# Padding stores one per step of the expert loop, and more buffers for its token numbers, gates and results

## The chip, the cores and the metric

The kernel runs on one core of one Trainium2 chip. The core's engines are TensorE (PE, with PEld for its weight loads), VectorE (DVE), ScalarE (ACT), GpSimd (POOL) and SyncE (SP, which here only issues transfers). Each engine works through its own instructions in order. The metric is the time of one execution in microseconds (us), and lower is better.

## What is computed

A Fourier mixer over 8 x 3072 tokens of width 256, a dense layer pair with a squared ReLU, and a layer of 8 experts in which each token goes to the one expert with the largest logit. The change touches the last part only:

```
def _moe2_ref(x, w_gate, w1, w2):
    logits = x @ w_gate
    expert_idx = np.argmax(logits, axis=1)
    probs = softmax(logits)                      # written out in the reference
    gate_w = probs[np.arange(N), expert_idx]
    for e in range(E):
        mask = expert_idx == e
        xe = x[mask]
        h = np.maximum(xe @ w1[e], 0.0)
        ye = h @ w2[e]
        out[mask] = gate_w[mask, None] * ye
```

N is 24,576 tokens, the width D is 256, E is 8 and the inner width of an expert is 1024. All is float32; the matmuls work on a high and a low part of each operand, three products to a matmul.

## The kernel before

The kernel has three stages that follow one another: the Fourier mixer, the dense layers, and the expert loop. The dense stage ends each tile of 384 tokens by computing the logits and writing each token's row to a table in DRAM, `bucket`, in the region of its expert. A row has 258 numbers: the 256 values, the gate, and the token's number. The region of an expert is filled from its start, so its last block of rows is only partly used.

The expert loop (`run`, L954) works on **slots**. A slot is a block of 512 rows of one expert (`ngr(s)` is 4, slots 0 to 40) or of 256 rows (`ngr(s)` is 2, slots 41 and on). A slot is worked in 4 or 2 **steps**. Each step of the loop does this, in program order:

- `e1` of the next step: the first expert matmuls, then ScalarE's `hh` (L872) and VectorE's `hl` (L873), the high and low parts of the hidden layer;
- one step of the side work (`_step(side)`, L959), until that is used up;
- on the first step of slot s: `prep_2(s + 1)`, the split of the second weights of the next slot, and `load(s + 3)`;
- `e2` of this step: the second expert matmuls (L892 to L894) into `acc`;
- on the last step of slot s: the results and their stores (below), then `prep_x(s + 2)` and `prep_1(s + 2)`.

`load(s)` issues three transfers on SyncE's queue: the slot's rows `xr` from `bucket` (L806), and the expert's weights `r1` (L812) and `r2` (L813). `prep_x(s)` copies the token numbers and gates out of `xr` on VectorE (`ids`, L823, and `gate`, L824), transposes the rows on TensorE and splits them. `ids` and `gate` come from the pool `p3`, which has three buffers for each name, so the copies for a slot take the buffers of three slots before.

The results of a slot are scaled by the gates on ScalarE into `ot` (L900). They go out by four (or two) indirect stores on GpSimd, one for each 128 rows (L902), which read `ot` and, as addresses, `ids`. `ot` shares its buffers with the `pay` of the dense stage; the pool `p2` has two of them.

The side work is one generator, `finish()`. It does the last tile of the dense stage (`gen_r`), then `table2` works out which rows the remaining slots hold, and ends with 16 **padding stores** (L746): indirect stores on GpSimd, two for each expert, that write 128 rows of `pad` each behind the last row of an expert's region. A padding row has a token number out of range, so that its result is not stored. Between the padding stores the generator yields after every second one, so that each step of the expert loop makes two. They write `bucket`, which the row loads read: a padding store waits for the one before it and for the row load issued before it, and a row load waits for the padding stores issued before it. The 16 stores are issued from the last step of slot 4 to the third step of slot 6.

Of the kernel before, what the change touches and what calls it, by code (L numbers as in the profile page):

```python
# [9 lines left out]
F32 = mybir.dt.float32  # L10
F32R = mybir.dt.float32r
F16 = mybir.dt.float16
I32 = mybir.dt.int32
# [6 lines left out]
D = 256  # L20
P = 128
# [6 lines left out]
ROW = D + 2  # L28
# [107 lines left out]
def kernel(  # L136
# [15 lines left out]
    def f32(ap):  # L152
        return ap.bitcast(F32)
# [52 lines left out]
    def ring():  # L206
        return psum["r"].tile([P, 512], F32, tag="r", name="r")
# [4 lines left out]
    def acc_tile():  # L212
        return psum["a"].tile([P, 1024], F32, tag="acc", name="acc")
# [322 lines left out]
    def x_tiles(k):  # L536
        p = spool["x"]
        xts[k] = (p.tile([P, 2, 512], F32R, tag="xth", name="xth"), p.tile([P, 2, 512], F32R, tag="xtl", name="xtl"))
        return xts[k]
# [42 lines left out]
    def moe():  # L582
# [4 lines left out]
        p2 = es.enter_context(tc.tile_pool(name="m2", bufs=2))  # L587
        p3 = es.enter_context(tc.tile_pool(name="m3", bufs=3))
# [63 lines left out]
        def row(name):  # L652
            return crow(name)[0:1]

        def tt(nm, shape):
            return p1.tile([1] + shape, F32, tag="tb_" + nm, name="tb_" + nm)
# [4 lines left out]
        def cumsum(dst, src):  # L661
            ltri = row("ltri").rearrange("o (a b) -> o a b", a=E)
            tmp = tt("tmp", [E, E])
            V.tensor_tensor(out=tmp, in0=ltri, in1=bc(src, 1, [E, E]), op=ALU.mult)
            V.tensor_reduce(out=dst, in_=tmp, axis=AX.X, op=ALU.add)

        def count(dst, src, thr, op):
            n = rowmap[thr][1]
            big = tt("big", [E, rowmap["thr"][1]])[:, :, 0:n]
            V.tensor_tensor(out=big, in0=bc(src, 2, [E, n]), in1=bc(row(thr), 1, [E, n]), op=op)  # L670
            V.tensor_reduce(out=dst, in_=big, axis=AX.X, op=ALU.add)
# [26 lines left out]
        def take(dst, avail, n):  # L698
            cum = tt("cum", [E])
            lim = tt("lim", [E])  # L700
            cumsum(cum, avail)
            V.tensor_scalar(out=lim, in0=cum, scalar1=float(n), scalar2=None, op0=ALU.min)
            V.tensor_copy(dst, lim)
            V.tensor_sub(dst[:, 1:E], lim[:, 1:E], lim[:, 0:E - 1])
            return lim
# [11 lines left out]
        def table2():  # L717
            te = tabs["te"]
            cnt, f, t2 = tt("cnt", [E]), tt("f", [E]), tt("t2", [E])
            V.tensor_sub(cnt, rbase[0:1], row("ecap"))  # L720
            count(f, cnt, "thr2", ALU.is_ge)
            yield
            V.tensor_sub(f, f, te)
            lim = take(t2, f, nf - nf1)
            yield
            yield from table(lim, t2, te, row("jf")[:, 0:nf - nf1], 512, nf1)
            V.tensor_add(te, te, t2)
            hc = tt("hc", [E])
            yield
            count(hc, cnt, "thr", ALU.is_gt)  # L730
            V.tensor_scalar(out=t2, in0=te, scalar1=-2.0, scalar2=None, op0=ALU.mult)
            V.tensor_add(hc, hc, t2)
            cum = tt("cum", [E])
            cumsum(cum, hc)
            V.tensor_scalar(out=slot_i[:, 2 * NS:2 * NS + 1], in0=cum[:, E - 1:E], scalar1=float(nf), scalar2=None, op0=ALU.add)
            yield
            yield from table(cum, hc, te, row("kh"), 256, nf)
            pf = p1.tile([P, E, 2], F32, name="padf", tag="padf")
            V.tensor_tensor(out=pf, in0=rbase.unsqueeze(2).to_broadcast([P, E, 2]),
                            in1=pidx.unsqueeze(1).to_broadcast([P, E, 2]), op=ALU.add)  # L740
            pint = p1.tile([P, 2 * E], I32, name="padi", tag="padi")
            V.tensor_copy(pint, pf.rearrange("p e i -> p (e i)"))
            for i in range(2 * E):
                if i % 2 == 0:
                    yield
                G.indirect_dma_start(  # L746
                    out=bucket[:, :], out_offset=bass.IndirectOffsetOnAxis(ap=pint[:, i:i + 1], axis=0),
                    in_=pad, in_offset=None)
# [24 lines left out]
        def g2(n, i):  # L773
            _, gh, gl = hid.pop((n, i))
            if i == 0:
                accs[n] = acc_tile()
            acc = accs[n]
            for f in range(2):
                fc = 2 * i + f
                for g in range(3):  # L780
                    o = acc[:, g * D:(g + 1) * D]
                    lh, ll = (t[:, f, g * P:(g + 1) * P] for t in (gh, gl))
                    st = fc == 0 and g != 1
                    T.matmul(o, lhsT=lh, rhs=woh[:, fc], start=st, stop=False, skip_group_check=True)  # L784
                    T.matmul(o, lhsT=lh, rhs=wol[:, fc], start=False, stop=False, skip_group_check=True)  # L785
                    T.matmul(o, lhsT=ll, rhs=woh[:, fc], start=False, stop=fc == 15, skip_group_check=True)  # L786
            if i == 7:
                pay = p2.tile([P, 4 * ROW], F32, tag="pay", name="pay")[:, :3 * ROW].rearrange("p (g c) -> p g c", g=3)
                acc = accs.pop(n)
                A.copy(pay[:, :, 0:D], acc[:, 0:3 * D].rearrange("p (g d) -> p g d", g=3))  # L790
                pays[n] = pay

        def ngr(s):
            return 4 if s < nf else 2

        def wset(s):
            hi, lo = (wih, woh) if s % 2 == 0 else (wil, wol)
            return hi[:, :, 0:F2], hi[:, :, F2:2 * F2], lo[:, 0:8], lo[:, 8:16]
# [17 lines left out]
        def prep_x(s, end):  # L816
            if s >= end:
                return
            k = ngr(s)
            xt = xr.pop(s)  # L820
            ids = p3.tile([P, 4], I32, tag="ids", name="ids")
            gate = p3.tile([P, 4], F32, tag="gate", name="gate")
            V.tensor_copy(ids[:, :k], xt[:, :, D + 1])  # L823
            V.tensor_copy(gate[:, :k], xt[:, :, D])  # L824
            meta[s] = ids, gate
            xh, xl = x_tiles(("s", s))
            for dc in range(2):
                ps = ring()
                for j in range(k):
                    T.transpose(ps[:, j * P:(j + 1) * P], xt[:, j, dc * P:(dc + 1) * P], ident)  # L830
                A.copy(xh[:, dc, :k * P], ps[:, :k * P])
                V.tensor_sub(xl[:, dc, :k * P], ps[:, :k * P], f32(xh[:, dc, :k * P]))
# [45 lines left out]
        def e2(s, i):  # L878
            k = ngr(s)
            nfc = 8 // k  # L880
            _, _, w2h, w2l = wset(s)
            hh, hl = (t.rearrange("p (f t) -> p f t", f=nfc) for t in hid.pop(("s", s, i)))
            if i == 0:
                accs["s", s] = acc_tile()
            acc = accs["s", s]
            for f in range(nfc):
                fc = nfc * i + f
                for g in range(k):
                    o = acc[:, g * D:(g + 1) * D]
                    lh, ll = (t[:, f, g * P:(g + 1) * P] for t in (hh, hl))  # L890
                    st = fc == 0 and g % 2 == 0
                    T.matmul(o, lhsT=lh, rhs=w2h[:, fc], start=st, stop=False, skip_group_check=True)  # L892
                    T.matmul(o, lhsT=lh, rhs=w2l[:, fc], start=False, stop=False, skip_group_check=True)
                    T.matmul(o, lhsT=ll, rhs=w2h[:, fc], start=False, stop=fc == 7, skip_group_check=True)  # L894
            if i == k - 1:
                ot = p2.tile([P, 4 * ROW], F32, tag="pay", name="ot")[:, :4 * D].rearrange("p (g d) -> p g d", g=4)
                acc = accs.pop(("s", s))
                ids, gate = meta.pop(s)
                for g in range(k):
                    A.activation(ot[:, g], acc[:, g * D:(g + 1) * D], AF.Copy, scale=gate[:, g:g + 1])  # L900
                for g in range(k):
                    ins = G.indirect_dma_start(  # L902
                        out=out, out_offset=bass.IndirectOffsetOnAxis(ap=ids[:, g:g + 1], axis=0),
                        in_=ot[:, g], in_offset=None, bounds_check=NT - 1, oob_is_err=False)
                    tc.declare_no_dep(ins.ins, group="out", reason="distinct rows")
                    tc.add_to_no_dep_group("out", ins.ins)
# [109 lines left out]
```

## Time and profile before

| | |
|---|---|
| median of 3 runs | 4155.14 us (4151.57 to 4155.75) |
| the profiled execution | 4157.26 us, of which the span from the first to the last instruction is 4155.4 us |
| TensorE matmul | 4027.7 us busy, 97% of the span |
| VectorE | 3097.2 us, 75% |
| ScalarE | 1970.8 us, 47% |
| GpSimd | 984.8 us, 24% |
| mean granted clock of TensorE | 0.989 of full speed |

The views are those of the hardware profiler for one execution. A timeline lists instructions with their start and duration; in brackets stands the idle time of the engine before the instruction and what ended it. A table of waits adds such idle times by instruction and releaser. A view by windows gives the busy time of each engine within a stretch, with the number of instructions. A transfer's issue shows as an instruction of the engine that issues it; when the data have landed is seen only from what waits for them. A wait for several things is put down to the one that came last. In the profile's rows the shape behind an output store is missing, since it is addressed by a list.

### The profile page before, as it was taken

What the parts mean: (1) busy time and instruction counts of PE and PEld (TensorE: products, weight loads), DVE (VectorE), ACT (ScalarE), POOL (GpSimd) and SP (SyncE); (2) the same over time, 40 slices, a digit from 0 to 9 for tenths busy, and PEclk for the clock granted to TensorE, in tenths of its full rate; (3) what the DMA queues carried; (4) which work ended last, traced back from release to release, by engine and by line L of the source; (5) the groups of instructions that cost most, each with busy time, mean ns of one, the idle gap of its engine ahead of it and who ended that gap; (6) DMA issues with size and microseconds to landing.
All of it is one profiled execution on the core that took longest, in us unless ns stands there. A gap on an engine that the chain in (4) does not pass through costs nothing. (4 is left out here: it accounts for less than half of the span.)

```text
span 4155.4 us, 72846 instructions
## 1 busy us (share of the span) xinstructions
PE 4027.7 (97%) x28092; PEld 3839.8 (92%) x28092; DVE 3097.2 (75%) x7513; ACT 1970.8 (47%) x3153; POOL 984.8 (24%) x715
## 2 busy tenths in 40 slices
PE   6988899999999999999999999999998999999998
PEld 3777788999999999999999999999998999999998
DVE  5999995788888888888888888888854545454465
ACT  3555555444444444444444444444443434343454
POOL 4655532111111111111111111111132222222232
PEclk7999999999999999999999999999999999999999
DMA  8876652000000000000000000000444444434364
GB/s 260 249 223 213 202 163 89 20 24 24 24 24 24 24 24 22 24 20 22 24 24 24 24 24 24 24 24 14 141 134 136 144 132 137 138 132 143 121 224 131
DMA packets 201779, 373.40 MB, mean 90 GB/s; under 512 B 18414, under 2 KB 128336, under 8 KB 201298
## 3 DMA queue, kind: packets, MB, share of 16 engines
q1 hardware_dynamic: 176578, 303.28, 23.3%
q0 software_dynamic: 23056, 59.11, 4.1%
q10 hardware_dynamic: 1792, 6.29, 0.5%
q8 instruction: 223, 3.65, 0.4%
q14 instruction: 130, 1.06, 0.1%
HBM read 259.08 MB, written 110.32 MB: 89 GB/s over the span
## 5 line engine op out<-in xcount | busy, mean ns | idle before, releaser
L784 PE MATMUL acc<-woh,gh 128*128 128x256 f32 x3072 | 884.3, 288 | 0.0
L764 ACT ACTIVATE rl<-g 128x768 f32<-128x768 f32 x512 | 415.8, 812 | 986.5 <-PE g L158 892.6
L785 PE MATMUL acc<-wol,gh 128*128 128x256 f32 x3072 | 864.6, 281 | 0.0
L786 PE MATMUL acc<-woh,gl 128*128 128x256 f32 x3072 | 858.5, 279 | 0.0
L156 PE MATMUL g<-xth,wih 128*128 128x384 f32 (+2 forms) x2512 | 857.7, 341 | 0.7 <-ACT gt L457 0.7
L157 PE MATMUL g<-xtl,wih 128*128 128x384 f32 (+2 forms) x2512 | 856.7, 341 | 0.0
L158 PE MATMUL g<-xth,wil 128*128 128x384 f32 (+2 forms) x2512 | 855.1, 340 | 0.0
L608 DVE CUSTOM_DVE_ANT_0 junk<-pay,wg 128x256 f32<-128x256 f32 x1536 | 650.8, 424 | 40.0
L771 DVE TENSOR_TENSOR gl<-sq,gh 128x768 fp32r<-128x768 f32 x512 | 612.9, 1197 | 32.1 <-DVE gh L770 0.9
L786 PEld LDWEIGHTS acc<-woh,gl 128*128 128x128 f32 x3072 | 580.7, 189 | 0.0
L784 PEld LDWEIGHTS acc<-woh,gh 128*128 128x128 f32 x3072 | 579.2, 189 | 0.0
L785 PEld LDWEIGHTS acc<-wol,gh 128*128 128x128 f32 x3072 | 577.8, 188 | 0.0
L873 DVE SCALAR_TENSOR_TENSOR hl<-g,hh 128x1024 fp32r<-128x1024 f32 x198 | 242.1, 1223 | 408.9 <-ACT hh L872 408.9
L553 POOL TENSOR_TENSOR hl<-ht,hh 96x1024 fp32r<-96x1024 f32 x64 | 154.4, 2413 | 1473.4 <-ACT hh L552 1473.4
L158 PEld LDWEIGHTS g<-xth,wil 128*128 128x128 f32 x2512 | 472.2, 188 | 13.6
L156 PEld LDWEIGHTS g<-xth,wih 128*128 128x128 f32 x2512 | 472.3, 188 | 11.9 <-ACT gt L457 1.4
L157 PEld LDWEIGHTS g<-xtl,wih 128*128 128x128 f32 x2512 | 472.7, 188 | 10.9
L872 ACT ACTIVATE hh<-g 128x1024 fp32r<-128x1024 f32 x198 | 203.4, 1028 | 565.3 <-PE g L158 540.0
L765 ACT ACTIVATE sq<-rl 128x768 f32<-128x768 f32 x512 | 433.6, 847 | 16.2
L902 POOL DMA_INDIRECT out_dram<-ot,ids x198 | 254.6, 1286 | 755.5 <-ACT ot L900 693.2
L770 DVE CAST gh<-sq 128x768 fp32r<-128x768 f32 x512 | 285.5, 558 | 79.6 <-ACT sq L765 73.3
L647 POOL DMA_INDIRECT bucket<-pay,pos x192 | 201.3, 1048 | 499.2 <-DMA bucket<-pay,pos 212.4
(192 smaller groups left out, 8351.9 us busy)
## 6 DMA issues: line engine op xcount, KB each, us to landing
r<-in_moe_w_dram SPq DMA_DIRECT2D x116, 1024.0 KB
xt<-in_x_dram SPq DMA_DIRECT2D x64, 384.0 KB
bt<-ad SPq DMA_DIRECT2D x96, 256.0 KB
gd<-gt SPq DMA_DIRECT2D x96, 256.0 KB
ht<-gd SPq DMA_DIRECT2D x64, 384.0 KB
xr<-bucket SPq DMA_DIRECT2D x41, 516.0 KB
ad<-at SPq DMA_DIRECT2D x48, 384.0 KB
tm<-tmd SPq DMA_DIRECT2D x72, 256.0 KB
```

Source lines behind the costliest of these rows:

```text
L156: T.matmul(ps, lhsT=lh, rhs=rh, start=first, stop=False)
L157: T.matmul(ps, lhsT=lh, rhs=rl, start=False, stop=False)
L158: T.matmul(ps, lhsT=ll, rhs=rh, start=False, stop=last)
L608: V.tensor_tensor_reduce(out=junk, in0=pay[:, g, 0:D], in1=wg[:, e], scale=1.0, scalar=0.0, op0=ALU.mult, op1=ALU.add, accum_out=lg[:, g, ...
L764: A.activation(r, ps[:, :, :TOK], AF.Relu)
L765: A.activation(g, r, AF.Square)
L770: V.tensor_copy(gh, g)
L771: V.tensor_sub(gl, g, f32(gh))
L784: T.matmul(o, lhsT=lh, rhs=woh[:, fc], start=st, stop=False, skip_group_check=True)
L785: T.matmul(o, lhsT=lh, rhs=wol[:, fc], start=False, stop=False, skip_group_check=True)
L786: T.matmul(o, lhsT=ll, rhs=woh[:, fc], start=False, stop=fc == 15, skip_group_check=True)
L902: ins = G.indirect_dma_start(out=out, out_offset=bass.IndirectOffsetOnAxis(ap=ids[:, g:g + 1], axis=0), in_=ot[:, g], in_offset=None, boun ...
```

## The change

The generator yields ahead of every padding store, so that each step of the expert loop makes one; `ids` and `gate` get six buffers instead of three; `pay` and `ot` get three instead of two.

```
             for i in range(2 * E):
-                if i % 2 == 0:
-                    yield
+                yield
                 G.indirect_dma_start(
...
             if i == 7:
-                pay = p2.tile([P, 4 * ROW], F32, tag="pay", name="pay")[:, :3 * ROW].rearrange("p (g c) -> p g c", g=3)
+                pay = p2.tile([P, 4 * ROW], F32, tag="pay", name="pay", bufs=3)[:, :3 * ROW].rearrange("p (g c) -> p g c", g=3)
...
-            ids = p3.tile([P, 4], I32, tag="ids", name="ids")
-            gate = p3.tile([P, 4], F32, tag="gate", name="gate")
+            ids = p3.tile([P, 4], I32, tag="ids", name="ids", bufs=6)
+            gate = p3.tile([P, 4], F32, tag="gate", name="gate", bufs=6)
...
             if i == k - 1:
-                ot = p2.tile([P, 4 * ROW], F32, tag="pay", name="ot")[:, :4 * D].rearrange("p (g d) -> p g d", g=4)
+                ot = p2.tile([P, 4 * ROW], F32, tag="pay", name="ot", bufs=3)[:, :4 * D].rearrange("p (g d) -> p g d", g=4)
```

The lines of the changed kernel behind L743 have a number that is one less. The order of instructions on TensorE, VectorE, ScalarE and SyncE is the same in both kernels; what moves is the order on GpSimd. Its instructions in the first slots of the expert loop stand so before the change. L647 are the last rows of the dense stage, L902 the output stores, four to a slot, and L746 the padding stores:

```order
L647 DMA bucket<-pay,pos 198912x258 x3
L902 DMA out_dram<-ot,ids 24576x256 x12
L746 DMA bucket<-pad,padi 198912x258 x2
L902 DMA out_dram<-ot,ids 24576x256 x4
L746 DMA bucket<-pad,padi 198912x258 x8
L902 DMA out_dram<-ot,ids 24576x256 x4
L746 DMA bucket<-pad,padi 198912x258 x6
L902 DMA out_dram<-ot,ids 24576x256 x140
```

And with the change:

```order
L647 DMA bucket<-pay,pos 198912x258 x3
L901 DMA out_dram<-ot,ids 24576x256 x12
L745 DMA bucket<-pad,padi 198912x258
L901 DMA out_dram<-ot,ids 24576x256 x4
L745 DMA bucket<-pad,padi 198912x258 x4
L901 DMA out_dram<-ot,ids 24576x256 x4
L745 DMA bucket<-pad,padi 198912x258 x4
L901 DMA out_dram<-ot,ids 24576x256 x4
L745 DMA bucket<-pad,padi 198912x258 x4
L901 DMA out_dram<-ot,ids 24576x256 x4
L745 DMA bucket<-pad,padi 198912x258 x3
L901 DMA out_dram<-ot,ids 24576x256 x132
```

The padding stores stand between the output stores of slots 3 to 8 as 1, 4, 4, 4 and 3, where they stood between those of slots 3 to 6 as 2, 8 and 6.

The second place is GpSimd's queue around the row load of slot 9, with what each instruction waits for. DMAHW2 is that row load, the DMASW names are earlier stores of GpSimd, Activation is ScalarE. Before the change, from slot 5's output stores to slot 6's second:

```order
L902 DMA out_dram<-ot,ids 24576x256 [waits Activation_49] x4
L746 DMA bucket<-pad,padi 198912x258 [waits DMASW6_49]
L746 DMA bucket<-pad,padi 198912x258 [waits DMASW3_49]
L746 DMA bucket<-pad,padi 198912x258 [waits DMAHW2_49,DMASW4_49]
L746 DMA bucket<-pad,padi 198912x258 [waits DMASW5_49]
L746 DMA bucket<-pad,padi 198912x258 [waits DMASW7_49,DMASW6_49]
L746 DMA bucket<-pad,padi 198912x258 [waits DMASW7_49,DMASW0_49]
L902 DMA out_dram<-ot,ids 24576x256 [waits DMASW1_49,DVE_49,Activation_49]
L902 DMA out_dram<-ot,ids 24576x256 [waits DMASW2_49,Activation_49]
```

And with the change, from slot 5's output stores to slot 6's first:

```order
L901 DMA out_dram<-ot,ids 24576x256 [waits DMASW2_49,Activation_49]
L901 DMA out_dram<-ot,ids 24576x256 [waits DMASW3_49,Activation_49]
L901 DMA out_dram<-ot,ids 24576x256 [waits DMASW4_49,Activation_49]
L901 DMA out_dram<-ot,ids 24576x256 [waits DMASW5_49,Activation_49]
L745 DMA bucket<-pad,padi 198912x258 [waits DMASW1_49]
L745 DMA bucket<-pad,padi 198912x258 [waits DMAHW2_49,DMASW6_49]
L745 DMA bucket<-pad,padi 198912x258 [waits DMASW7_49]
L745 DMA bucket<-pad,padi 198912x258 [waits DMASW0_49]
L901 DMA out_dram<-ot,ids 24576x256 [waits DMASW2_49,DVE_49,Activation_49]
```

The padding store that waits for slot 9's row load was the third of a run of six, and is now the second of a run of four. With the change the row loads of slots 8 to 12 each wait for a padding store; before it those of slots 8 to 10 did.

## Rows read from the trace of the kernel before

**Rows 1.** Busy time by engine, whole span: us, share, instructions.

```profile
PE 4027.7 (97%) x28092; PEld 3839.8 (92%) x28092; DVE 3097.2 (75%) x7513; ACT 1970.8 (47%) x3153; POOL 984.8 (24%) x715
```

**Rows 2.** Busy time by stage: window, length, PE, PEld, DVE, ACT, POOL; clock, DMA share, GB/s.

```profile
3091.00:3163.00 72.00, 72.00 (x471) 65.57 (x469) 34.04 (x37) 30.46 (x45) 25.11 (x23) 1.00 0.33 112
3163.00:3197.00 34.00, 23.36 (x147) 21.40 (x146) 11.43 (x15) 7.83 (x10) 7.89 (x8) 0.85 0.58 190
3197.00:3997.00 800.00, 800.00 (x5345) 735.01 (x5344) 401.11 (x465) 333.33 (x462) 196.97 (x143) 1.00 0.43 141
```

**Rows 3.** TensorE's waits from 2985 us to the end: total us, times, longest.

```profile
PE acc L894 <- DVE hl L873: 10.6, 1, 10.6
```

**Rows 4.** TensorE's timeline, 3169 to 3185 us: start, duration, instruction; idle before it, releaser.

```profile
3169.83 0.28 PE L893 MATMUL acc<-woh,hh 128*128 128x256 f32 x1
3180.75 0.58 PE L894 MATMUL acc<-woh,hl 128*128 128x256 f32 x1 [10.64 <-DVE hl L873]
...
3183.69 0.41 PE L892 MATMUL acc<-woh,hh 128*128 128x256 f32 x1
```

**Rows 5.** Busy time of two neighbouring slots, columns as in rows 2.

```profile
3160.69:3196.32 35.63, 24.99 (x154) 22.74 (x153) 11.43 (x15) 9.46 (x13) 8.87 (x9) 0.86 0.55 181
3196.32:3219.61 23.29, 23.29 (x154) 21.24 (x153) 11.39 (x13) 9.48 (x14) 5.43 (x4) 1.00 0.42 137
```

**Rows 6.** VectorE's timeline, 3158 to 3180 us, columns as in rows 4.

```profile
3158.91 1.22 DVE L873 SCALAR_TENSOR_TENSOR hl<-g,hh 128x1024 fp32r<-128x1024 f32 x1 [4.38 <-ACT hh L872]
3175.26 0.17 DVE L823 CAST ids<-xr 128x4 int32<-128x4 f32 x1 [15.12 <-DMA out_dram<-ot,ids]
...
3179.48 1.22 DVE L873 SCALAR_TENSOR_TENSOR hl<-g,hh 128x1024 fp32r<-128x1024 f32 x1
```

**Rows 7.** ScalarE's timeline, the results of slots 5, 6 and 7.

```profile
3114.11 1.57 ACT L900 ACTIVATE ot<-acc,gate 128x256 f32<-128x256 f32 x4 [1.81 <-PE acc L894]
...
3138.11 1.57 ACT L900 ACTIVATE ot<-acc,gate 128x256 f32<-128x256 f32 x4 [2.52 <-PE r L830]
...
3160.69 1.57 ACT L900 ACTIVATE ot<-acc,gate 128x256 f32<-128x256 f32 x4 [1.81 <-DMA bucket<-pad,padi]
```

**Rows 8.** GpSimd's timeline, 3091 to 3167 us.

```profile
3091.58 0.99 POOL L902 DMA_INDIRECT out_dram<-ot,ids  x1 [2.33 <-ACT ot L900]
...
3095.96 1.97 POOL L902 DMA_INDIRECT out_dram<-ot,ids  x1 [0.30 <-issue]
3098.23 1.95 POOL L746 DMA_INDIRECT bucket<-pad,padi  x1 [0.30 <-issue]
...
3109.48 0.97 POOL L746 DMA_INDIRECT bucket<-pad,padi  x1 [5.93 <-DMA xr<-bucket]
3116.53 0.97 POOL L746 DMA_INDIRECT bucket<-pad,padi  x1 [6.09 <-DMA bucket<-pad,padi]
3119.55 1.64 POOL L746 DMA_INDIRECT bucket<-pad,padi  x1 [2.05 <-DMA bucket<-pad,padi]
...
3130.81 0.99 POOL L902 DMA_INDIRECT out_dram<-ot,ids  x1 [0.30 <-issue]
...
3146.48 0.97 POOL L746 DMA_INDIRECT bucket<-pad,padi  x1 [5.89 <-DMA xr<-bucket]
3153.74 0.97 POOL L746 DMA_INDIRECT bucket<-pad,padi  x1 [6.29 <-DMA bucket<-pad,padi]
...
3161.71 0.97 POOL L746 DMA_INDIRECT bucket<-pad,padi  x1 [2.36 <-DMA bucket<-pad,padi]
3162.99 0.99 POOL L902 DMA_INDIRECT out_dram<-ot,ids  x1 [0.31 <-ACT xth L831]
...
3166.88 0.98 POOL L902 DMA_INDIRECT out_dram<-ot,ids  x1 [0.30 <-issue]
```

**Rows 9.** SyncE's queue, row loads of slots 8 and 9.

```profile
3105.48 0.35 SPq L806 DMA_DIRECT2D xr<-bucket  x1
...
3142.46 0.35 SPq L806 DMA_DIRECT2D xr<-bucket  x1
```

## The prediction

> **What bounds the kernel now.** I read the busy totals first. TensorE works 97% of the span, VectorE 75%, everything else less [rows 1], so an edit that adds no TensorE work can only gain where TensorE stands still or runs slowly. Neither the padding stores nor the buffers touch a matmul, so the second view is busy time by stage, over the stretch in which the padding stores are made and the expert loop behind it [rows 2]. From 3091 to 3163 us TensorE is busy 72.00 of 72.00 us, from 3197 to 3997 us it is busy 800.00 of 800.00; between them, from 3163 to 3197 us, only 23.36 of 34.00, with a granted clock of 0.85 instead of 1.00. So there is one hole. The table of TensorE's waits says the same: from 2985 us to the end one wait is worth counting, 10.6 us, on VectorE's hl [rows 3].
>
> The timeline then shows the hole itself [rows 4]: a matmul starts at 3169.83, the next at 3180.75 after 10.64 us of idling. What follows takes 0.41 us for each matmul, against 0.28 for the same form before, until about 3184: after the idle time the engine ran at the lower of its two levels, 1.2 GHz instead of 2.4.
>
> The price of the hole is read from two neighbouring slots of the expert loop, cut where ScalarE begins a slot's results [rows 5]. The slot with the hole takes 35.63 us, the next 23.29 us, both with 154 matmuls recorded. The difference is 35.63 - 23.29 = **12.34 us**, of which 35.63 - 24.99 = 10.64 us is idling and 24.99 - 23.29 = 1.70 us is slower running.
>
> Now the chain backwards. VectorE made its hl of the previous step at 3158.91, then stood 15.12 us at the copy of token numbers (ids, L823), which an output store released, and made the late hl at 3179.48 [rows 6]. The copy for slot 9 writes the buffer of slot 6, since there are three, so it needs slot 6's four output stores. ScalarE had begun slot 6's results at 3138.11 [rows 7], but GpSimd issued the first of their stores at 3162.99, **24.9 us** later, and the last at 3166.88 [rows 8]. In between GpSimd sent slot 5's stores (from 3130.81) and a run of six padding stores, the last of them at 3161.71. GpSimd takes its instructions in order, and each padding store waits for the one before it to land, or for a row load. Slot 5's results, begun at 3114.11, had waited for the eight padding stores ahead of them in the same way. So the cause is a queue: fourteen padding stores, in two runs, ahead of stores whose buffers VectorE wants back.
>
> **The change, part by part.** *One padding store per step.* The same 16 stores are issued, at the same price each, and the queue on GpSimd reads 1, 4, 4, 4, 3 between the groups of output stores instead of 2, 8, 6. How long is a group of four? From the first output store of a slot (3091.58) to the end of the fourth (3095.96 + 1.97) is 6.35 us, a padding store follows 0.30 later, and a row load is issued 2.9 us after the padding store it waits for (I take the spacing of two padding stores that wait on one another, 3119.55 - 3116.53 = 3.02, as its upper bound and 2.9 as the value). That puts the load at 6.35 + 0.30 + 2.9 = 9.55 us after the slot's first output store. The next padding store came 4.0 us after the load (3105.48 to 3109.48), the one behind it 7.05 later, the third 3.02 later, and 1.27 us after that GpSimd is free (0.97 for the issue, 0.30 between) [rows 8, 9]. Sum: 9.55 + 4.0 + 7.05 + 3.02 + 1.27 = 24.9 us per slot against a slot of 23.29 us. The output stores thus fall behind by 1.6 us per slot, and over the three full groups by about 5 us, not by 24.9.
>
> *Six buffers for ids and gate.* The copy for slot s+2 now waits for the output stores of slot s-4, three slots (3 x 23.29 = 69.9 us) older than before. Even with the old queue slot 3's stores were out long before 3158.91, since GpSimd sent slot 4's at 3091.58. So each of these two parts alone would take most or all of the 15.12 us away, and together their gain is counted once.
>
> *Three buffers for results (pay, ot).* ScalarE's results of slot s wait for the stores of slot s-3 instead of s-2. In the trace slot 6's results start 24.00 us after slot 5's and slot 7's 22.58 us after that [rows 7]; the two sum to 2 x 23.29, so the 0.7 us was given back and TensorE never saw it. I count zero, between 0 and 0.7. The buffers are also used in the stage before the expert loop; nothing there waits on a result buffer in TensorE's rows, so zero there too.
>
> *What is late next.* With the ids copy free, VectorE could begin slot 9's preparation at about 3160.1 (3158.91 plus the 1.22 us of hl). The rows of slot 9 had been asked for at 3142.46 and were in by 3146.48, when the padding store that waited for them started [rows 8, 9]. Nothing else in the hole is late, so the loop should go on at 23.29 us a slot as it does behind 3197 us.
>
> *Sum.* The profiled execution took 4157.26 us (span 4155.4), 2.1 us above the median of the runs, 4155.14. Against itself: 4157.26 - 12.34 = 4144.9; put on the median: 4155.14 - 12.34 = **4142.8**, say 4143 us, 0.30% less. Bounds of the terms: the idling alone, if the slower running came back elsewhere, is 10.64, giving 4144.5; the hole plus the 0.7 us above gives 4142.1. The runs before spread from 4151.57 to 4155.75, so the lowest less the full gain is 4139.2.
>
> **Rivals.** *The hole stays (within 0.2%).* The change might not do what it says: the copy of ids waits for the load of its rows as well as for stores, and a wait for several is put down to the one that came last. If the rows' load or the weights behind it were the real cause, the hole would move to the next line of VectorE and the time would stay 4155. Against it: the rows of slot 9 had landed 13 us before VectorE stood still, and VectorE's own next hl came 4.2 us after the release [rows 6, 8]. For it: a row load now waits for a padding store in five slots running, where before it was three. A middle case, in which half of the hole returns as shorter waits, gives 4155.1 - 6.2 = 4149.
>
> *Slower: the row loads become the bound.* Each slot's row load now sits behind a padding store that sits behind the previous slot's output stores, and the two weight loads sit behind it on the same in-order queue. With a mean spacing t behind a load, a slot on GpSimd takes 9.55 + 4.0 + 1.27 + 2t = 14.82 + 2t us, so the fourth load is late by 9.55 + 3 x (14.82 + 2t - 23.29). The rows are needed at the end of the following slot, 46.58 us after its usual start; the spacing was back to 3.02 at 3119.55, 14.1 us after the load at 3105.48, by which I take the weights to have arrived, so the slack is 46.58 - 14.1 = 32.5 us. At the measured mean t = 5.0 the lateness is 14 us. TensorE would wait from t = 8.1 on, the gain would be eaten at about t = 10, and the kernel would be 0.2% (8.3 us) slower from t = 11.5. At t = 12 the wait is 23.6 us and the time 4155.1 - 12.3 + 23.6 = 4166. The longest spacing in my rows is 7.26 (3146.48 to 3153.74) [rows 8].
>
> What could stretch t is VectorE: the padding store at 3098.23, issued amid VectorE's weight preparation, took 1.95 us on GpSimd, against 0.97 at 3109.48 and 3116.53 [rows 8]. In the new order one store of each group stands at that place. If all of them took the 0.98 us more, on top of the longest spacing, t would be 7.26 + 0.98 = 8.24, the fourth load 33.6 us late, TensorE's wait 1.1 us and the time 4144. That is still the forecast. The Trainium skill has a rule that speaks against the change here (SBUF — State Buffer, "SBUF: two separate sides"): GpSimd cannot write a DMA's descriptors while VectorE runs certain copies, and a DMA of some 620 ns then takes some 3100. The 1.95 agrees with it in direction, at a factor of two. With that page's 2.5 us more for each, an estimate, t would be 9.8, TensorE's wait 10 us and the time 4153, so that the gain would be paid back; I count 0.02 for it, within the case that the time does not move.
>
> **How the numbers follow.** Forecast, the hole gone: 0.78. The hole stays or half of it returns: 0.18 (about 0.06 of it the half). Slower by the row loads: 0.04. Differences under about 0.2% (8.3 us, so from 4146.8 to 4163.4) can hardly be told from no change here. Faster is the forecast, 0.78; same 0.18; slower 0.04. The range runs from 4139, the lowest run less the full gain, to 4149, the half case; it leaves out the full hole (0.12), the slower case (0.04), and a few in a hundred below.
>
> **What would show it.** In the changed kernel no wait of VectorE on ids of more than 1 us; no wait of TensorE over 1 us behind 2985 us; five groups of padding stores, the first output store of each slot at most about 10 us behind ScalarE's results; row loads of those slots 10 to 15 us late and harmless; the granted clock 1.00 through the stretch; the slot of 35.63 us at 23.3. I am wrong if a slot in that stretch still takes over 24 us, or if the hole is gone and the end does not come 12 us earlier.

## The result, and the profile after

The changed kernel takes **4116.23 us** (median, 4114.52 to 4116.98). Run beside it, the kernel before takes 4153.93 (4151.57 to 4155.75), and the ratio is 0.9908, with an interval of 0.9897 to 0.992. That is 37.7 us less, and three times the 12.3 us that were forecast; it lies 23 us below the range. The profiled execution took 4116.9 us, with a span of 4115.1 and a mean granted clock of 0.990 (before 4155.4 and 0.989), so its span is 40.3 us shorter.

**The hole is gone.** TensorE's waits from 2940 us to the end (line waited for: us in total, times, longest) no longer hold an entry on hl; [rows 3] had one of 10.6 us. These are the first of them in the changed kernel:

```profile
PE r L829 <- DVE pb L642: 1.1, 2, 0.9
PE acc L892 <- DVE woh L850: 0.9, 1, 0.9
```

VectorE's waits over the same stretch begin as follows. None is on ids, where [rows 6] had 15.12 us:

```profile
DVE hl L872 <- ACT hh L871: 398.8, 136, 4.4
DVE xtl L831 <- ACT xth L830: 117.8, 56, 2.5
DVE gh L769 <- ACT sq L764: 1.2, 2, 0.8
```

ScalarE's timeline shows the results of four slots in the stretch where the padding stores are made, and of the slot behind them; it answers to [rows 7]. Columns: start, duration, instruction, idle before it and its releaser.

```profile
3097.50 1.57 ACT L899 ACTIVATE ot<-acc,gate 128x256 f32<-128x256 f32 x4 [1.72 <-PE acc L893]
...
3120.37 1.57 ACT L899 ACTIVATE ot<-acc,gate 128x256 f32<-128x256 f32 x4 [1.73 <-PE acc L893]
...
3143.60 1.57 ACT L899 ACTIVATE ot<-acc,gate 128x256 f32<-128x256 f32 x4 [1.80 <-PE acc L893]
...
3166.47 1.57 ACT L899 ACTIVATE ot<-acc,gate 128x256 f32<-128x256 f32 x4 [1.73 <-PE acc L893]
...
3189.70 1.57 ACT L899 ACTIVATE ot<-acc,gate 128x256 f32<-128x256 f32 x4 [1.80 <-PE acc L893]
```

GpSimd's timeline between them, to be read beside [rows 8]:

```profile
3082.04 1.95 POOL L745 DMA_INDIRECT bucket<-pad,padi  x1 [0.30 <-issue]
3090.05 0.97 POOL L745 DMA_INDIRECT bucket<-pad,padi  x1 [6.05 <-DMA xr<-bucket]
3097.65 0.97 POOL L745 DMA_INDIRECT bucket<-pad,padi  x1 [6.64 <-DMA bucket<-pad,padi]
3100.54 1.04 POOL L745 DMA_INDIRECT bucket<-pad,padi  x1 [1.92 <-DMA bucket<-pad,padi]
3101.89 1.59 POOL L901 DMA_INDIRECT out_dram<-ot,ids  x1 [0.30 <-issue]
...
3126.67 1.00 POOL L901 DMA_INDIRECT out_dram<-ot,ids  x1 [0.30 <-issue]
...
3150.99 1.99 POOL L901 DMA_INDIRECT out_dram<-ot,ids  x1 [0.30 <-issue]
...
3172.71 1.00 POOL L901 DMA_INDIRECT out_dram<-ot,ids  x1 [0.30 <-issue]
```

The first output store comes 4.4, 6.3, 7.4 and 6.2 us behind ScalarE's results (3101.89 - 3097.50 and so on), where it was up to 24.9 before. So far the forecast describes what happened. Now the slots: 3120.37 - 3097.50 = 22.87 us, then 23.23, then 22.87. None of them is 23.29, which was the undisturbed slot before.

**The rest is in the pace of TensorE.** I cut both traces at ScalarE's copies that end a dense tile (pay) and a slot (ot). From the start to the end of the first dense tile it is 1.4 us less (730.33 to 728.89), which is no effect of the change: the two runs below that move no operand of TensorE have 732.65 and 727.93 there. The 63 intervals between tiles take 2227.82 us instead of 2241.36, so 13.5 less. The expert loop from its first to its last results takes 1114.99 instead of 1139.93, so 24.9 less, of which 12.34 is the hole [rows 5] and 12.6 shorter slots elsewhere. The busy time by engine does not point there, since TensorE stands at 97% as in [rows 1], but its sum is 28.5 us smaller for the same 28,092 instructions:

```profile
PE 3999.2 (97%) x28092; PEld 3815.1 (93%) x28092; DVE 3096.0 (75%) x7513; ACT 1970.1 (48%) x3153; POOL 987.5 (24%) x715
```

Windows of one dense tile and of two slots show it best. Columns as in [rows 2]: window, length, then busy time and number of instructions of PE, PEld, DVE, ACT and POOL, the clock, the DMA share, GB/s. Before:

```profile
1015.07:1050.67 35.60, 35.60 (x260) 35.44 (x259) 29.36 (x93) 17.35 (x27) 5.39 (x4) 1.00 0.08 23
3336.04:3382.61 46.57, 46.57 (x306) 42.47 (x305) 22.77 (x26) 18.95 (x26) 10.86 (x8) 1.00 0.44 136
```

After:

```profile
1011.91:1047.29 35.38, 35.38 (x260) 35.22 (x259) 29.38 (x93) 17.34 (x28) 5.62 (x4) 1.00 0.08 24
3328.00:3374.10 46.10, 46.10 (x306) 42.09 (x305) 22.77 (x26) 18.93 (x26) 10.86 (x8) 1.00 0.42 138
```

TensorE is busy all of the window in both, at full clock, with 260 matmuls recorded to a tile and 306 to two slots; only the time is shorter. Which matmuls? The timeline of TensorE over one step's second expert matmuls (24 of them), in a slot that uses woh. Before, its first and last and the next matmul:

```profile
3409.33 0.28 PE L892 MATMUL acc<-woh,hh 128*128 128x256 f32 x1
...
3412.05 0.28 PE L894 MATMUL acc<-woh,hl 128*128 128x256 f32 x1
3412.16 0.39 PE L156 MATMUL g<-xth,wih 128*128 128x512 f32 x1
```

After:

```profile
3423.63 0.28 PE L891 MATMUL acc<-woh,hh 128*128 128x256 f32 x1
...
3426.26 0.28 PE L893 MATMUL acc<-woh,hl 128*128 128x256 f32 x1
3426.38 0.39 PE L156 MATMUL g<-xth,wih 128*128 128x512 f32 x1
```

Before, 2.83 us for 24, or 118 ns from one to the next; after, 2.75 us, or 114.6 ns. A single matmul's duration of 0.28 tells nothing of that, since they overlap. Before, the spacing was 118.1 ns on average in the slots with woh and in those with wol. After, it is 114.4 in those with woh and 117.8 in those with wol, almost what it was, and that is the alternation of 22.87 and 23.23. A step of a slot with wol, after:

```profile
3400.39 0.28 PE L891 MATMUL acc<-wol,hh 128*128 128x256 f32 x1
...
3403.10 0.28 PE L893 MATMUL acc<-wol,hl 128*128 128x256 f32 x1
3403.22 0.40 PE L156 MATMUL g<-xth,wil 128*128 128x512 f32 x1
```

These 24 take 2.83 us. In the dense stage the second matmuls behind the matmuls of c_dft went from 2.19 to 2.14 us for 18, the others from 2.13 to 2.12.

TensorE's order of instructions is the same in both kernels, and so are its data. What differs is **where the data lie**. `pay` and `ot` are tiles of 4128 bytes in each partition, which is 4096 + 32. A third one pushes everything that the pools place behind it by 4128 bytes: `r1` and `r2`, and the hidden layers that TensorE reads, `gh`/`hh` from 153792 to 157920 and `gl`/`hl` from 166080 to 170208 (start addresses from the two built programs). The weights `wih`, `wil`, `woh`, `wol` and the rows `xth`, `xtl` stay. `ids` and `gate` lie behind all of these, so that six of them move nothing that TensorE reads. The expectations below call the operand that PEld loads ahead of a matmul stationary (in the second expert matmuls hh and hl) and the other one moving (there woh and wol); in the first they are wih or wil, and xth and xtl.

### The profile page after: what moved, and what is told of

It reads as the page before. It is cut to its first block, busy times and chain, and to the rows that moved or that the text cites. A ratio compares the mean times of both kernels' runs of the same rounds, so it can differ in the third digit from the quotient of the medians.

```text
span 4115.1 us, 72845 instructions
## 1 busy us (share of the span) xinstructions
PE 3999.2 (97%) x28092; PEld 3815.1 (93%) x28092; DVE 3096.0 (75%) x7513; ACT 1970.1 (48%) x3153; POOL 987.5 (24%) x715
## 5 line engine op out<-in xcount | busy, mean ns | idle before, releaser
L647 POOL DMA_INDIRECT bucket<-pay,pos x192 | 201.6, 1050 | 494.8 <-DMA bucket<-pay,pos 211.1
```

## The experiments

All numbers are medians in us; a ratio is to the kernel before, run on the same chip beside it. Its median was 4153.9 for the runs of the three parts and the 32-byte gap, and between 4152.86 and 4153.97 for the later ones. "Tile" is the interval between dense tiles, "slot" that between full slots outside the hole, both cut as above.

### The three parts, one at a time

The kernel before with the padding stores alone:

```diff
             for i in range(2 * E):
-                if i % 2 == 0:
-                    yield
+                yield
```

> Only the padding stores are one per step; all buffers as before. The changed kernel was 37.7 us faster, of which the hole explains 12.3; the rest, some 25 us, is a shorter spacing of TensorE's matmuls (dense tile 35.59 to 35.38 us, full expert slot 23.29 to 23.05 on average). Address theory: the third results buffer moved gh, gl, hh and hl by 4128 bytes in SBUF, and their place sets the spacing. Then this kernel keeps 35.59 and 23.29 us, loses the hole and is 12 us faster, about 4142. Waits theory: the order of GpSimd's stores or a freed buffer shortens the spacing; then part of the 25 us may come with this edit, down to 4116 if it is all of it.

With six buffers for ids and gate alone:

```diff
-            ids = p3.tile([P, 4], I32, tag="ids", name="ids")
-            gate = p3.tile([P, 4], F32, tag="gate", name="gate")
+            ids = p3.tile([P, 4], I32, tag="ids", name="ids", bufs=6)
+            gate = p3.tile([P, 4], F32, tag="gate", name="gate", bufs=6)
```

> Only ids and gate have six buffers. They lie behind gl and hl in SBUF, so nothing that TensorE reads moves. My prediction said that this part alone takes the hole away: 12 us faster, about 4142, with a tile of 35.59 and a slot of 23.29 us as before. If the hole has another cause it stays and the time is 4154. Address theory: spacing unchanged. Waits theory: spacing could change here, towards 4116.

With three buffers for the results alone:

```diff
-                pay = p2.tile([P, 4 * ROW], F32, tag="pay", name="pay")[:, :3 * ROW].rearrange("p (g c) -> p g c", g=3)
+                pay = p2.tile([P, 4 * ROW], F32, tag="pay", name="pay", bufs=3)[:, :3 * ROW].rearrange("p (g c) -> p g c", g=3)
...
-                ot = p2.tile([P, 4 * ROW], F32, tag="pay", name="ot")[:, :4 * D].rearrange("p (g d) -> p g d", g=4)
+                ot = p2.tile([P, 4 * ROW], F32, tag="pay", name="ot", bufs=3)[:, :4 * D].rearrange("p (g d) -> p g d", g=4)
```

> Only pay and ot have three buffers, which moves gh, gl, hh and hl by 4128 bytes. The hole of 12 us should stay, since ids still has three buffers and the padding stores are in their old order. Address theory and the theory that the third buffer itself frees ScalarE both expect the short spacing: tile 35.38, slot 23.05 on average, 25 us faster, about 4129. If neither holds, 4154.

| part alone | time (range) | ratio | tile | slot |
|---|---|---|---|---|
| padding stores | 4142.33 (4141.73 to 4147.18) | 0.9975 [0.9966, 0.9985] | 35.59 | 23.29 |
| ids and gate | 4142.54 (4140.73 to 4143.28) | 0.9973 [0.9964, 0.9983] | 35.59 | 23.29 |
| results | 4126.68 (4125.74 to 4127.54) | 0.9937 [0.992, 0.9953] | 35.38 | 22.86 / 23.24 |

With the padding stores alone, and likewise with ids and gate alone, no wait of TensorE behind 2940 us is longer than 0.9 us. The longest of TensorE's waits with the padding stores alone:

```profile
PE acc L892 <- DVE woh L850: 0.9, 1, 0.9
```

Each of the two takes the whole hole away by itself and leaves the pace of the slots at 23.28 to 23.29: 11.6 us (4153.9 - 4142.33) and 11.4 us against 12.34 read from [rows 5]. In the traces the expert loop, cut as above, takes 1127.63 and 1127.62 us, 12.3 less than the 1139.93 before. The third part leaves the hole in place, as its first entry among TensorE's waits shows,

```profile
PE acc L894 <- DVE hl L873: 9.4, 1, 9.4
```

and still brings 27.2 us, with the shorter tile and the alternating slots of the changed kernel. The parts add up: 27.2 and the hole once, 11.6, make 38.8, against 37.7 measured for all three. The hole is a little smaller in the kernel with the results alone, where the loop takes 1126.03 us, 11.0 more than in the changed kernel.

### A buffer that nobody uses

If the third result buffer helps because results need not wait, an unused tile must do nothing. If it helps because it moves what lies behind it, 32 unused bytes should do what it does, since 4128 is 4096 + 32. The kernel before, with one unused tile in front of `gh` and `gl` (pool `m3`; r1 and r2 lie ahead of it and stay):

```diff
         p3 = es.enter_context(tc.tile_pool(name="m3", bufs=3))
+        p3.tile([P, 8], F32, name="gap", tag="gap", bufs=1)
```

> The kernel before with an unused tile of 32 bytes ahead of gh in its pool: gh, gl, hh, hl, ids and gate move by 32 bytes, nothing else changes. 4128 is 4096 + 32. If the low part of the address sets the spacing, this gives the short spacing (35.38 and 23.05 us) with the hole still there, about 4129 us. If the 4096 matter, or the third buffer itself, it stays at 4154.

4126.83 (4125.94 to 4127.13), ratio 0.9937 [0.9921, 0.9954]. The tile and two slots of it, columns as above, and its longest wait of TensorE behind 2940 us:

```profile
3338.09:3384.19 46.10, 46.10 (x306) 42.09 (x305) 22.77 (x26) 18.95 (x27) 10.87 (x8) 1.00 0.44 138
```

```profile
PE acc L895 <- DVE hl L874: 8.3, 1, 8.3
```

Two slots in 46.10 us, to the hundredth what the changed kernel takes, with two result buffers, three for ids, and the hole still there. Besides gh, gl, hh and hl only ids and gate move with the gap, and the dense stage, whose tile is the shorter one too, uses neither. This settles it for the third part: **it gains by moving the operands, not by letting results go earlier.** The same with 64 and 96 unused bytes (`[P, 16]` and `[P, 24]` in place of `[P, 8]`):

> The kernel before with an unused tile of 64 bytes ahead of gh. gh, gl, hh and hl then start at a multiple of 64 again, as in the kernel before; the moving operands woh and wol start 32 bytes behind one. If the place within 64 bytes sets the spacing, it is the long one: tile 35.59, full slot 23.29 us, about 4154. If any move away from the old address helps, or the period is 128 bytes, the short one: 35.38 and 23.05, about 4127.

> The same with 96 bytes: gh starts 32 bytes behind a multiple of 64, as with the gap of 32, but 32 behind a multiple of 128 where that one is at 96. With a period of 64 the short spacing, about 4127, the same as the gap of 32. With a period of 128 something else, 4154 or below 4127.

64 bytes gave 4155.21 (4153.8 to 4160.81), ratio 1.0006 [0.9996, 1.0017], tile 35.71, slot 23.21: a longer tile, a shorter slot and a smaller hole (its slot takes 31.84 us) come out even. 96 bytes gave 4168.48 (4167.2 to 4169.98), ratio 1.0037 [1.0024, 1.005], the slowest of all, although its hole is smaller too (32.74 us). Its tile and two of its slots:

```profile
1013.78:1049.56 35.78, 35.78 (x260) 35.62 (x259) 29.36 (x93) 17.36 (x28) 5.40 (x4) 1.00 0.07 23
3342.67:3389.39 46.72, 46.72 (x306) 42.59 (x305) 22.77 (x26) 18.95 (x26) 10.86 (x8) 1.00 0.43 136
```

The same instructions again, 0.40 us longer to a tile and 0.62 to two slots than in the changed kernel, by an unused tile alone.

### Is it a distance or a place?

The next kernels start from the changed one and move other operands too: the weights, by an unused tile ahead of them; the rows `xth` and `xtl`, by one behind them in a pool that is filled from the other end (its other tiles, as the loaded rows `xr`, move along, and so do the high and low parts that the c_dft matmuls of the dense stage read). The last is the fastest kernel of this study; its edit:

```diff
     slot_i = const.tile([1, 2 * (nf + nh) + 1], I32, name="slot_i")
+    const.tile([P, 8], F32, name="gap0")
...
         xts[k] = (p.tile([P, 2, 512], F32R, tag="xth", name="xth"), p.tile([P, 2, 512], F32R, tag="xtl", name="xtl"))
+        if k == 0:
+            p.tile([P, 24], F32, tag="gapx", name="gapx", bufs=1)
         return xts[k]
```

The first line alone, then the first line with the 32-byte gap ahead of gh, then this edit:

> The changed kernel with an unused tile of 32 bytes ahead of the weights: wih, wil, woh, wol and also gh, gl, hh, hl move by 32 bytes, so that all of them start at a multiple of 64; xth and xtl stay 32 bytes behind one. Same-half theory: a matmul's spacing is short where its stationary and its moving operand start in the same half of 64 bytes. Then the second matmuls keep the short spacing and the first ones, whose operands now differ, get longer: from 4116 up. Stationary theory: only the stationary operand's start counts, and a start at a multiple of 64 is slow: the second matmuls go back to 118 ns, about 4143 or, with wih now at a multiple of 64 too, more.

> The changed kernel with wih, wil, woh and wol moved by 32 bytes to a multiple of 64 and gh, gl, hh, hl left 32 bytes behind one. Same-half theory: both the first and the second matmuls have operands in different halves, the second go back to 118 ns, about 4143 or more. Stationary theory: the second matmuls keep the short spacing, the first change with wih.

> The changed kernel with the weights, gh, gl, hh and hl moved up by 32 bytes, as in the run with moved weights, and xth and xtl moved too, by -96 bytes, which is +32 modulo 128. Counting start addresses modulo 128, so far the spacing was shortest where stationary and moving operand are 64 apart, longer at 32 and 96, longest at 0. Distance theory: all distances are those of the changed kernel again, so the time is 4116, tile 35.38, slot 23.05 us. Fixed-place theory: gh at a multiple of 128 was slow with the gap of 64 and xth has a new place, so the time stays near the 4140 of the run with moved weights or goes up.

Only the rows moved by 64 bytes (`[P, 16]` in gapx, no gap0), and a 128-byte gap ahead of gh in the changed kernel (`[P, 32]`):

> The changed kernel with xth and xtl moved by -64 bytes alone, so that the first matmuls have stationary and moving operand at the same place modulo 128; the second matmuls are untouched. Distance theory: the first matmuls get their longest spacing, slower than with 32 apart (4140), so 4145 to 4170; the second keep theirs. Otherwise 4116.

> The changed kernel with an unused tile of 128 bytes ahead of gh: gh, gl, hh and hl move by 128 bytes. If the period is 128 bytes nothing changes, 4116 within 3 us, tile 35.38. If it is 256 or more, another time, by the size of the other runs 4120 to 4160 or below 4110.

The fastest kernel with a 256-byte gap ahead of gh as well, and with all operands 64 bytes further (`[P, 24]` in gap0, `[P, 72]` in gapx):

> The fastest kernel so far (all operands moved by 32 bytes, xth and xtl by -96; 4108.5 us, tile 35.31 us) with gh, gl, hh and hl moved by 256 bytes more. The 128 of the last run made the changed kernel 22 us slower, so the period is not 128. If it is 256 bytes, this stays at 4108 within 3 us with a tile of 35.31 us; if it is longer, 4115 to 4150.

> The fastest kernel so far with every operand of the expert and dense matmuls moved by 64 bytes modulo 256: weights and gh, gl, hh, hl by +64, xth and xtl by -192. All distances between operands, modulo 256, are kept, all places change. Distance theory: 4108 within 3 us, tile 35.31, full slot 22.97 us. Fixed-place theory: another time, by the other runs 4115 to 4150.

Here are all kernels in the order of their start addresses, each given as the remainder by 256; the low parts and the second weights have the remainders of their partners. The first six differ in gh alone among these operands.

| kernel | weights, gh, xth | time (range) | tile | slot |
|---|---|---|---|---|
| before | 160, 192, 224 | 4153.9 (4149.2 to 4156.2) | 35.59 | 23.29, one hole |
| before + 32 | 160, 224, 224 | 4126.83 (4125.94 to 4127.13) | 35.38 | 22.86 / 23.24, one hole |
| changed | 160, 224, 224 | 4116.23 (4114.52 to 4116.98) | 35.38 | 22.87 / 23.23 |
| before + 64 | 160, 0, 224 | 4155.21 (4153.8 to 4160.81) | 35.71 | 23.21, one hole |
| before + 96 | 160, 32, 224 | 4168.48 (4167.2 to 4169.98) | 35.78 | 23.30 / 23.43, one hole |
| changed + 128 | 160, 96, 224 | 4138.2 (4136.74 to 4140.05) | 35.53 | 23.20 to 23.33 |
| weights + 32 | 192, 0, 224 | 4139.68 (4136.15 to 4142.5) | 35.53 | 23.37 |
| weights + 32, gh + 32 | 192, 32, 224 | 4156.98 (4154.05 to 4160.61) | 35.73 to 35.80 | 23.30 / 23.41 |
| rows - 64 | 160, 224, 160 | 4136.36 (4134.42 to 4137.37) | 35.53 | 23.19 |
| weights + 32, rows - 96 | 192, 0, 128 | **4108.49** (4108.0 to 4109.09) | 35.31 | 22.96 |
| the same, gh + 256 | 192, 0, 128 | 4110.09 (4108.81 to 4112.08) | 35.31 | 22.96 |
| the same, all + 64 | 0, 64, 192 | 4111.37, 4113.38; 4136.46 to 4140.64 | 35.36 | 22.97 |

gap0 also moves gh, as it moves all that lies behind it. What follows:

- A shift of gh by 256 bytes costs nothing beyond 1.6 us, a shift by 128 costs 22 us. So the remainder by 128 does not decide, and the one by 256 is a candidate.
- Putting the distance between gh and the weights back does not put the time back: "weights + 32" has gh - weights = 64 as the changed kernel has, and takes 23 us more. Adding 32 to gh as well makes it worse. The third operand, xth, counts too: "rows - 64" moves neither gh nor the weights and costs 20 us. Its trace shows the effect where I had not looked for it: the second expert matmuls, which do not read xth at all, went to 117.8 ns in every slot. A step of a slot with woh there, to be set beside the 2.75 us of the changed kernel:

```profile
3399.93 0.28 PE L893 MATMUL acc<-woh,hh 128*128 128x256 f32 x1
...
3402.64 0.28 PE L895 MATMUL acc<-woh,hl 128*128 128x256 f32 x1
3402.76 0.40 PE L156 MATMUL g<-xth,wil 128*128 128x512 f32 x1
```

  These 24 take 2.83 us. So the time is not decided by the two operands of one matmul alone.
- The fastest kernel has the short spacing in both kinds of slot (113.8 and 113.9 ns), though its first expert matmuls are no faster: 12 of them take 2.79 us, against 2.75 to 2.77 in the changed kernel. Its tile and two slots:

```profile
1043.36:1078.68 35.32, 35.32 (x260) 35.16 (x259) 29.34 (x93) 17.38 (x28) 5.51 (x4) 1.00 0.07 24
3319.75:3365.68 45.93, 45.93 (x306) 41.68 (x305) 22.75 (x26) 18.96 (x27) 10.86 (x8) 1.00 0.43 139
```

  It beats both kernels: ratio 0.9894 [0.9878, 0.9911] to the kernel before, and 7.7 us less than the changed one. It was found by trying, not by a rule: neither of the two theories in its expectation gave 4108.
- The last kernel keeps all distances of the fastest and moves every place by 64. Two of its six executions took 4111.37 and 4113.38, which speaks for distances; four took 4136.46 to 4140.64, which speaks against them alone. The granted clock is 0.989 to 0.991 in all six. One program then has two paces, some 26 us apart. The profile fell on the execution of 4113.38, so what is longer in the others was not seen.

## Why the prediction was wrong, by its own steps

- **The hole and its price: right.** 35.63 - 23.29 = 12.34 us was read; 11.6 and 11.4 were measured with each remedy alone. That each part by itself takes the stall away and that the gain counts once was said and held. That the idling and the slower running after it both go was said, and held too: 12.3 us less in the loop with either remedy alone.
- **The queue on GpSimd: right in its sizes.** The prediction had the first output store at most about 10 us late (measured 4.4 to 7.4) and a mean spacing behind a row load of 5.0 us (measured, from 3090.05 to 3097.65 and 3100.54: 7.60 and 2.89, so 5.2; 5.0 and 5.1 in the next two groups). The row loads of SyncE's queue in the same stretch:

```profile
3086.03 0.35 SPq L805 DMA_DIRECT2D xr<-bucket  x1
...
3111.17 0.35 SPq L805 DMA_DIRECT2D xr<-bucket  x1
...
3135.45 0.35 SPq L805 DMA_DIRECT2D xr<-bucket  x1
...
3160.73 0.35 SPq L805 DMA_DIRECT2D xr<-bucket  x1
...
3174.74 0.35 SPq L805 DMA_DIRECT2D xr<-bucket  x1
...
3190.57 0.35 SPq L805 DMA_DIRECT2D xr<-bucket  x1
```

  The last of these comes 0.9 us behind its slot's results (3189.70), so that this is the undisturbed place. Against it the first four are 10.5, 12.8, 14.2 and 16.3 us late, where 9.6 to 14 was reckoned, and the fifth, behind the group of three, 7.4. TensorE waited for none of them, as its window from slot to slot shows (columns as in [rows 2]):

```profile
3074.65:3189.70 115.05, 115.05 (x762) 105.06 (x761) 56.96 (x65) 47.34 (x65) 41.43 (x35) 1.00 0.46 155
```

- **Both rivals stayed away.** The hole did not move to another line, and the row loads did not become the bound; of the slack of 32.5 us half was used. The store amid VectorE's weight preparation took 1.95 us as before (at 3082.04), and none of GpSimd's stores in the stretch over 1.99. The prediction was wrong to set the 1.95 beside the rule it weighed there (the Trainium skill, SBUF — State Buffer, "SBUF: two separate sides"). That rule is about certain operations of VectorE, copies among them, and from 620 to 3100 ns it gives a factor of five. Beside the store at 3082.04, as beside the one at 3098.23 before, VectorE was subtracting, not copying, so these rows do not test the rule:

```profile
3081.93 1.22 DVE L850 TENSOR_TENSOR woh<-r,woh 128x1024 fp32r<-128x1024 f32 x1
```

  They show a factor of two at most, and only beside such subtractions: in the changed kernel, from 3100 to 3950 us, the 75 indirect stores that ran beside VectorE's subtractions for the weights took 1.68 us on average, and none of the 87 others over 1.31.
- **The step that failed: "an edit that adds no TensorE work can only gain where TensorE stands still or runs slowly".** I took 100% busy at full clock as a pace that cannot change. It says only that the matmuls follow one another without a gap; how far apart they start is another number, and it went from 118 to 114 ns in half of the second expert matmuls. From this came the second mistake, the term for three buffers for results, "I count zero, between 0 and 0.7". It measured 27.2 us. I looked at who waits for a buffer and not at where the buffer is put. The two kernels' addresses could have been compared before the prediction; they would have said that operands move, not by how much or which way the time moves. That it went down was luck: 96 bytes in place of 32 made the kernel slower.
- **"The loop should go on at 23.29 us a slot": wrong for the same reason.** It went on at 22.87 and 23.23, and the dense stage, where I had counted zero, gave 13.5 us.
- **The range** ended at the lowest run less the full gain, so it had room for noise and none for a term that I had not priced. Kernels with the same work and another memory layout have run here between 4108 and 4157 without the hole, and up to 4168 with it; an edit that moves tiles should have had a range that admits it.

What stays open: which rule ties the addresses to the spacing, why the short spacing alternates with the slots of woh and wol in the changed kernel though both weights have the same remainder, why moving xth changes matmuls that do not read it, and what the two paces of the last kernel are. ScalarE and VectorE write gh, gl, hh and hl, and TensorE reads them; whether the place matters to the reading or to the writing was not separated. I have shown that moving gh, gl, hh and hl (and with them only ids and gate) moves the time by 27 us down (32 bytes) or 15 us up (96 bytes); by what part of the chip, I have not.

## What to carry to other kernels

Where TensorE is busy without a gap, measure its pace by the interval between two equal points (tile to tile) and compare that between kernels, since the busy share cannot show it. A change of a buffer count or of a tile's size is also a change of every address behind it: before crediting the buffer, run the kernel with an unused tile of the same size, or of its odd bytes, in its place. And in a kernel that TensorE bounds it is cheap to try a few unused tiles of 32 to 96 bytes ahead of the operands; here that was worth more than the waits. No run shows that the same places help another kernel.

## What was unexpected of the hardware

Moving SBUF tiles in steps of 32 bytes changes the spacing of back-to-back matmuls whose work, order and clock are the same: 113.8 to 118.6 ns for the second expert matmuls of 128x256 in the kernels above, 35.31 to 35.80 us for a dense tile, 4108 to 4168 us for the kernel, the hole included where there is one. One program (the last experiment) ran at two paces, 4111 to 4113 and 4136 to 4141 us, with the same addresses in all of its executions, so the addresses alone do not fix the pace in every case.
